# Attention feeding two feed-forward layers on one core: products with v as two halves of 64 columns, sums of the probabilities on GpSimd and by way of DMAs, preparation in fixed slots

## The chip, the cores and the metric

One core of one Trainium2 chip. The metric is the device time of one execution in microseconds (us). The engines are TensorE (PE; PEld is its weight load), VectorE (DVE), ScalarE (ACT), GpSimd (POOL) and SyncE (SP), which here only issues DMAs.

## The reference: what is computed

Attention with a mask by clusters, and two feed-forward layers on its output (numpy, cut):

```python
# q, k, v: (2, 8, 768, 64); centroids: (8, 16, 64)
q_assign = argmax(einsum('bhsd,hcd->bhsc', q_n, c_n), axis=-1)   # q_n, c_n: normalised rows
k_assign = argmax(einsum('bhsd,hcd->bhsc', k_n, c_n), axis=-1)
mask = q_assign[:, :, :, None] == k_assign[:, :, None, :]
scores = where(mask, q @ k.T / 8, -1e9)
attn = exp(scores - max(scores));  attn = attn / (sum(attn) + 1e-9)
x = (attn @ v) as (1536, 512)
h = maximum(x @ w_in, 0);  x = h * h @ w_out          # layer 1: 512 -> 2048 -> 512
h = x @ w2_in;  out = h * cos(h) @ w2_out             # layer 2
```

## The kernel before

The 16 (batch, head) problems go as 8 **pairs** of heads; the two heads of a pair (`j`) lie in partitions 0 to 63 and 64 to 127. Every engine's order is written out by hand: Python loops append instructions, and each engine runs its own list in order.

**Steps.** The main loop counts `g`. At step `g`, `scores(g)` makes the scores of one tile of 128 keys against 384 queries (half a head, `HALF`) for both heads: 8 products on TensorE, each on one half of the array's rows, then one `exp` on ScalarE into a tile `p` (L400). In the same step `s_max(g + 9)` (`LEAD` is 9) makes scores of a later tile in the other orientation (L350), and VectorE takes row maxima of them (L353). A pair is 12 steps, so the loop has 96 with scores. On odd steps `pv` multiplies two finished tiles `p` with `v`.

**Banks.** Scores, maxima and every preparation share three PSUM `unit`s, handed out in turn. A step's use of a unit waits for whoever read it three uses earlier, in most cases the maximum of the step before (DVE) or the `exp` (ACT).

**pv before.** `p` is the stationary operand (128 keys x 128 queries), `vv` the moving one: 64 columns of v and one column of ones, so that column 65 collects the sum of the probabilities. Both heads and three query tiles lie side by side in one bank `o_ps[hf]`, which a product with `zeros` opens. `divide` (7 steps after a half begins) adds 1e-9 to the sums, inverts them and multiplies on VectorE. `combine` (a step later) transposes the result on TensorE; ScalarE writes the high part `xh`, VectorE the rest `xl`.

**Preparation** of a pair (`prep`, a table by step): load q and k, squares and sums (`norm_sq`, `norm_sum`), 14 small VectorE instructions for the inverse norms (`norm_inv`), transposes (`transpose_in`) with two copies on ScalarE (`h` rounded, `f` exact), the remainder (`low_part`), similarities to the centroids in f32 (`sims`), the argmax as one-hot rows (`cluster`, `one_hot`), and DMAs that lay rows into `xq`, `xk`, `yk`, which `s_max` and `scores` read.

**Weights.** Each feed-forward weight is split into two parts by 6 VectorE instructions and an ACT copy (`w_split`, L135 to L144). The first 7 half-tiles (`n_early`) are loaded and split during attention, one instruction a step; the other 25 of layer 1 are loaded after `att.close()`, when attention's buffers are given back, and are split during the first 15 steps of the layer.

Of the kernel before, what the change touches and what calls it, by code (L numbers as in the profile page):

```python
# [33 lines left out]
def tile_kernel(ctx: ExitStack, tc: tile.TileContext, q, k, v, centroids, w1i, w1o, w2i, w2o, out):  # L34
# [22 lines left out]
    ps = ctx.enter_context(tc.tile_pool(name="ps", bufs=1, space=PSUM))  # L57

# [10 lines left out]
    zeros = perm.tile([P, 2 * HT * (D + 1)], BF16, name="zeros")  # L69
    nc.gpsimd.memset(zeros, 0.0)  # L70
# [107 lines left out]

    vv = [ap.tile([P, NT, 2, D + 1], F32, name=f"vv{i}") for i in range(2)]

    def load_raw(n, names):
        b, hp = pairs[n]
        for nm in names:
            if nm == "v":
                t = vv[n % 2][:, :, :, :D]
            else:
                t = prepp.tile([P, NT, 2, D], F32, tag=f"raw{nm}", name=f"raw{nm}{n}", bufs=2)
            src = {"q": q, "k": k, "v": v}[nm]
            for j in range(2):
                nc.sync.dma_start(t[:, :, j, :], src[b, 2 * hp + j].rearrange("(p t) d -> p t d", t=NT))  # L190
            raw[n, nm] = t
# [49 lines left out]
    def transpose_in(n, x):  # L241
        d = pd[n]
        u = unit()
        for t in range(NT):
# [3 lines left out]
            )  # L248
        d["h" + x] = ap.tile([P, S], F32R, tag="h" + x, name=f"h{x}{n}", bufs=3)
        d["f" + x] = prepp.tile([P, S], F32, tag="f" + x, name=f"f{x}{n}")  # L250
        d["l" + x] = ap.tile([P, S], F32R, tag="l" + x, name=f"l{x}{n}", bufs=3)
        nc.scalar.copy(halves(d["h" + x]), wide(u))
        nc.scalar.copy(halves(d["f" + x]), wide(u))
        d["t" + x] = u
# [67 lines left out]
    def one_hot(n):  # L322
        d = pd[n]
        u = unit()
        for t in range(NT):
# [4 lines left out]
            )  # L330
        ot = prepp.tile([2 * GC, S], F32R, tag="ot", name=f"ot{n}")
# [424 lines left out]
```

## Time and profile before

| | |
|---|---|
| median of 3 runs | 990.65 us (987.68 to 992.36) |
| the profiled execution | 982.26 us, of which the span is 980.5 us |
| PE busy | 917.2 us, 94% of the span |
| DVE busy | 601.8 us, 61% |
| ACT busy | 366.7 us, 37% |
| POOL busy | 28.3 us, 3% |
| mean granted TensorE clock | 0.926 of full speed |

The profiled execution is 0.85% below the median. Busy shares are averages over stages with different limits: preparation of the first pair (to about 29 us), the pairs of attention (to about 405 us), and the two layers.

### The profile page before, as it was taken

The page shows a single profiled execution, that of the slowest core. Times are in us where ns is not written, and L with a number is a line of the kernel's source. Part 1 is how long each engine was busy: PE and PEld are TensorE (multiplying, and loading weights), DVE is VectorE, ACT ScalarE, POOL GpSimd, SP SyncE. Part 2 cuts the span into 40 slices and gives each one's busy share as a digit, 9 for nine tenths or more (in the row PEclk, how much of TensorE's full clock was granted, in tenths as well). Part 3 has the DMA queues.
Part 4 walks back from the last instruction along what each step waited for, and adds up shares of the span by engine and source line. Part 5 has one row for each costly group of instructions (what it writes and reads, how often), then busy time and mean ns, then how long its engine had stood idle before and what let it go on. Part 6 is the DMA issues. An engine that isn't in the chain of part 4 may idle for free.

```text
span 980.5 us, 12966 instructions
## 1 busy us (share of the span) xinstructions
PE 917.2 (94%) x5097; PEld 759.4 (77%) x5097; DVE 601.8 (61%) x1159; ACT 366.7 (37%) x580; POOL 28.3 (3%) x58
## 2 busy tenths in 40 slices
PE   5699999999999999999879999999899999999997
PEld 5488888888888888887568888887677778887886
DVE  6775656453545442299972112899899885666655
ACT  2252525251525233344433334444433343333332
POOL 4000000000000000010000000000012000000000
PEclk6587979795979799999999999999999999999999
DMA  8240313121211110590000001665200010001001
GB/s 239 57 90 13 78 25 66 29 62 29 61 25 34 29 30 9 179 357 1 1 1 1 1 0 47 192 192 173 85 1 1 1 43 1 1 1 43 0 1 43
DMA packets 65934, 54.89 MB, mean 56 GB/s; under 512 B 40784, under 2 KB 58192, under 8 KB 65872
## 3 DMA queue, kind: packets, MB, share of 16 engines
q1 hardware_dynamic: 65872, 54.05, 19.5%
q8 instruction: 40, 0.66, 0.3%
q14 instruction: 22, 0.18, 0.1%
HBM read 43.02 MB, written 3.15 MB: 47 GB/s over the span
## 4 chain that ended last, share of the span: by engine, by line
PE 64%; DVE 25%; ACT 4%; issue 4%; DMA 3%; SPq 0%; POOL 0%; DVEq 0%; ACTq 0%
PE unit L503 17%; PE o_ps L418 15%; PE unit L396 10%; PE unit L564 8%; PE o_ps L564 7%; DVE top L143 3%; PE unit L350 3%; DVE aux L141 3%; DVE aux L144 2%; PE unit L279 2%; DVE ewr L542 2%; ACT p L400 2%; DVE w L136 2%; DMA wraw<-in_moe_w_out_dram 2%; DVE aux L140 2%
## 5 line engine op out<-in xcount | busy, mean ns | idle before, releaser
L503 PE MATMUL unit<-xh,w 128*128 128x512 f32 x768 | 258.2, 397 | 15.1 <-DVE ews L525 9.8
L503 PEld LDWEIGHTS unit<-xh,w 128*128 128x128 f32 x768 | 144.7, 189 | 55.9 <-DVE ews L525 13.7
L418 PEld LDWEIGHTS o_ps<-vv,p 128*128 128x128 f32 x1152 | 151.1, 212 | 8.5 <-issue 8.4
L418 PE MATMUL o_ps<-vv,p 128*128 128x65 f32 x1152 | 154.3, 296 | 0.0
L503 PE MATMUL unit<-xl,w 128*128 128x512 f32 x384 | 151.8, 395 | 0.0
L400 ACT ACTIVATE p<-unit 128x768 f32<-128x768 f32 x96 | 77.8, 813 | 184.3 <-PE unit L396 178.8
L353 DVE TENSOR_REDUCE m<-unit 128x2 f32<-128x768 f32 x96 | 91.4, 952 | 87.5 <-PE unit L350 87.3
L542 DVE TENSOR_TENSOR ewr<-ews,ewr 128x512 fp32r<-128x512 f32 x83 | 57.0, 687 | 79.0 <-ACT ewr L520 77.0
L503 PEld LDWEIGHTS unit<-xl,w 128*128 128x128 f32 x384 | 72.5, 189 | 15.6
L564 PE MATMUL unit<-ewr,w 128*128 128x512 f32 x288 | 76.7, 402 | 6.9 <-ACT w L135 6.9
L564 PE MATMUL unit<-w,ewr 128*128 128x512 f32 x288 | 75.1, 395 | 1.0 <-DVE ewr L542 1.0
L564 PE MATMUL o_ps<-ewr,w 128*128 128x512 f32 x288 | 75.7, 399 | 0.0
L564 PE MATMUL o_ps<-w,ewr 128*128 128x512 f32 x288 | 74.7, 394 | 0.0
L529 ACT ACTIVATE ews<-ews,hpi 128x512 f32<-128x512 f32 x48 | 34.8, 724 | 96.7 <-DVE ews L528 96.7
L564 PEld LDWEIGHTS unit<-ewr,w 128*128 128x128 f32 x288 | 53.5, 189 | 22.3 <-ACT w L135 9.4
L135 ACT CAST w<-top 128x512 fp32r<-128x512 f32 x64 | 39.7, 620 | 75.6 <-DVE top L143 74.1
L564 PEld LDWEIGHTS o_ps<-ewr,w 128*128 128x128 f32 x288 | 55.1, 191 | 13.4
L564 PEld LDWEIGHTS unit<-w,ewr 128*128 128x128 f32 x288 | 54.0, 188 | 14.3 <-DVE ewr L542 1.4
L537 DVE TENSOR_TENSOR ews<-unit,ews 128x512 f32<-128x512 f32 x48 | 33.2, 691 | 51.2 <-ACT ews L533 45.2
L564 PEld LDWEIGHTS o_ps<-w,ewr 128*128 128x128 f32 x288 | 54.1, 188 | 13.0
L518 ACT ACTIVATE ews<-unit 128x512 f32<-128x512 f32 x48 | 28.7, 598 | 86.9 <-PE unit L503 86.9
L396 PE MATMUL unit<-hq,hk 64*128 64x384 f32 x192 | 46.0, 476 | 13.4 <-DVE m L353 10.9
(145 smaller groups left out, 1148.0 us busy)
## 6 DMA issues: line engine op xcount, KB each, us to landing
wraw<-in_moe_w_in_dram SPq DMA_DIRECT2D x32, 512.0 KB, 4.5
wraw<-in_moe_w_out_dram SPq DMA_DIRECT2D x32, 512.0 KB, 4.2
rawq<-in_q_dram SPq DMA_DIRECT2D x16, 192.0 KB, 4.1
rawk<-in_k_dram SPq DMA_DIRECT2D x16, 192.0 KB, 4.3
vv<-in_v_dram SPq DMA_DIRECT2D x16, 192.0 KB, 3.2
out_dram<-outs SPq DMA_DIRECT2D x12, 256.0 KB, 2.2
xk<-hk SPq DMA_DIRECT2D x16, 96.0 KB, 2.1
xq<-lq SPq DMA_DIRECT2D x16, 96.0 KB, 2.2
```

The source lines that it names most:

```text
L135: nc.scalar.copy(w[:, 0], top.bitcast(F32))
L141: cost(690, lambda: ve.scalar_tensor_tensor(restf, low, 2.0**-32, rest, ALU.mult, ALU.add)),
L143: cost(690, lambda: ve.scalar_tensor_tensor(top, high, 0xC0000000, top, ALU.bitwise_and, ALU.bitwise_or)),
L353: nc.vector.tensor_reduce(d["m"][:, i, :, kh], u[:, :, :HALF], AX, ALU.max)
L396: nc.tensor.matmul(u[:, j, :HALF], lhsT=a[r, ks], rhs=b[r, qs], start=(p == 0), stop=(p == len(ops) - 1))
L400: nc.scalar.activation(t, u[:, :, :HALF], AF.Exp, scale=SCALE)
L418: nc.tensor.matmul(o[:, i, j], lhsT=t[:, j, i * P : (i + 1) * P], rhs=vv[n % 2][:, kt, j], start=False, stop=(kt == NT - 1 and i == HT - 1 ...
L503: nc.tensor.matmul(ph, lhsT=w[:, a, :], rhs=x[blk][:, a, :], start=(a == i == 0), stop=(a == KD - 1 and i == 2))
L529: nc.scalar.activation(e2, e2, AF.Sin, bias=hpi)
L537: nc.vector.tensor_tensor(e2, ph, e2, ALU.mult)
L542: e.tensor_tensor(al, e2, ah.bitcast(F32), ALU.subtract)
L564: nc.tensor.matmul(y, lhsT=a, rhs=b, start=(f == 0 and i == 0), stop=(f == NF - 1 and i == 2))
```

## The change

It does five things.

1. `pv` takes v as the stationary operand (64 columns of one head) and `p` as the moving one (384 queries). Head 0 writes partitions 0 to 63 of `o_ps[hf]`, head 1 partitions 64 to 127. There is no column of ones, no `zeros`, and no transpose in `combine`.
2. `add_up` adds the six tiles `p` of a half on GpSimd into `acc` (5 additions of 128x768). `sums` multiplies `acc` with a tile of ones; `move_sums` copies the result (ACT) and DMAs a row of it over 32 partitions; `invert` works on the 64x12 numbers, DMAs them to DRAM, and DMAs each row back over 64 partitions (`rb`). `divide` is one multiplication, 13 steps after the half begins. `xl` is made on GpSimd.
3. `sims` works on `h` and `l` parts: three products per tile in place of an f32 one, q and k in one unit. The copies `f` go.
4. The preparation has slots within a step (PRE: ahead of the scores, PROD: behind pv, POST: last), and starts 5 steps earlier.
5. `n_early` is 8. Early splits run one instruction a step up to step 0, then 2 in 5 steps; late ones by a rule that gives two half-tiles to each of the layer's steps 2 to 10 and one to steps 11 to 16.

```diff
     def load_raw(n, names):
...
-                t = vv[n % 2][:, :, :, :D]
+                t = ap.tile([P, NT, 2, D], F32, tag="rawv", name=f"rawv{n}", bufs=2)
...
-    def sims(n, x):
...
+    def sims(n):
+        d = pd[n]
+        u = d["sim"] = unit()
+        hp = pairs[n][1]
+        for i, x in enumerate("qk"):
+            for t in range(NT):
+                ts = slice(t * P, (t + 1) * P)
+                for p, (a, c) in enumerate(((d["h" + x], cbh), (d["l" + x], cbh), (d["h" + x], cbl))):
+                    nc.tensor.matmul(
+                        u[:, i, t * GC : (t + 1) * GC], lhsT=a[:, ts], rhs=c[:, hp, :], start=(p == 0), stop=(p == 2)
+                    )
...
+    def add_up(u_):
+        hb, kt = divmod(u_, NT)
+        if kt == 0:
+            return
+        if kt == 1:
+            accs[hb] = ap.tile([P, 2, HALF], F32, tag="acc", name=f"acc{hb}", bufs=2)
+            nc.gpsimd.tensor_tensor(accs[hb], ptiles[u_ - 1], ptiles[u_], ALU.add)
+        else:
+            nc.gpsimd.tensor_tensor(accs[hb], accs[hb], ptiles[u_], ALU.add)
 
     def pv(u_):
...
-        for i in range(HT):
-            for j in range(2):
-                nc.tensor.matmul(
-                    o[:, i, j], lhsT=t[:, j, i * P : (i + 1) * P], rhs=vv[n % 2][:, kt, j],
-                    start=False, stop=(kt == NT - 1 and i == HT - 1 and j == 1),
-                )
+        for j in range(2):
+            nc.tensor.matmul(
+                o_ps[hf][j * D : (j + 1) * D, :HALF], lhsT=raw[n, "v"][:, kt, j, :], rhs=t[:, j],
+                start=(kt == 0), stop=(kt == NT - 1),
+            )
+    def sums(hb):
+        u = su[hb] = unit()
+        acc = accs.pop(hb)
+        for j in range(2):
+            nc.tensor.matmul(u[j * D : (j + 1) * D, 0, :HALF], lhsT=ones, rhs=acc[:, j], start=True, stop=True)
+    def move_sums(hb):
+        u = su.pop(hb)
+        t = ap.tile([P, HALF], F32, tag="st", name=f"st{hb}")
+        nc.scalar.copy(t, u[:, 0, :HALF])
+        give(u)
+        r = inv[hb] = ap.tile([2 * R, GR], F32, tag="r", name=f"r{hb}", bufs=2)
+        for j in range(2):
+            nc.sync.dma_start(r[j * R : (j + 1) * R], t[j * D : j * D + 1].rearrange("o (p c) -> o p c", c=GR))
+    def invert(hb):
+        b, hp = pairs[hb // 2]
+        r = inv.pop(hb)
+        nc.vector.tensor_scalar(r, r, 1e-9, None, ALU.add)
+        nc.vector.reciprocal(r, r)
+        row = dram.tile([2, HALF], F32, tag="row", name=f"row{hb}", bufs=2)
+        nc.sync.dma_start(row.rearrange("j (p c) -> (j p) c", c=GR), r)
+        rb = rbs[hb] = ap.tile([P, HALF], F32, tag="rb", name=f"rb{hb}", bufs=2)
+        for j in range(2):
+            nc.sync.dma_start(rb[j * D : (j + 1) * D], row[j : j + 1, :].broadcast_to([D, HALF]))
     def divide(hb):
-        o = o_view(hb % 2)
...
+        x = xs[hb] = ap.tile([P, HALF], F32, tag="x", name=f"x{hb}", bufs=2)
+        nc.vector.tensor_tensor(x, o_ps[hb % 2][:, :HALF], rbs.pop(hb), ALU.mult)
...
             nc.scalar.copy(dst, src)
-            nc.vector.tensor_tensor(xl[blk][:, hp, off : off + w], src, dst.bitcast(F32), ALU.subtract)
+            nc.gpsimd.tensor_tensor(xl[blk][:, hp, off : off + w], src, dst.bitcast(F32), ALU.subtract)
...
-                for i in range(1 + (idx % 3 != 1)):
+                for i in range(-(-len(to_split[0]) // (NF + 1 - idx))):
...
+    prep = [
+        (-22, PRE, load_raw, "qk"),
+        (-17, PROD, transpose_in, "q"),
...
+        (-13, PRE, norm_sum, "k"),
+        (-12, PRE, norm_inv),
+        (-11, PROD, transpose_in, "k"),
+        (-10, PRE, high_part, "k"),
+        (-10, POST, low_part, "k"),
+        (-9, PROD, sims),
+        (-8, PRE, scale_sims),
+        (-7, PRE, cluster, 0, 1),
+        (-6, PRE, cluster, 1, 3),
+        (-5, PRE, cluster, 3, 4),
+        (-4, PRE, cluster, 4, 5),
+        (-3, PRE, stage),
+        (-3, PROD, one_hot),
+        (-2, PRE, stage_oh),
...
+    finish = [
+        (8, PROD, sums),
+        (9, PRE, move_sums),
+        (11, PRE, invert),
+        (13, PRE, divide),
+        (13, POST, combine),
+    ]
```

**TensorE, the products of a pair in the middle of attention.** `p` are tiles of probabilities, `hq` to `yk` the operands of scores (L396, now L411) and maxima (L350, now L360), `xt` the divided result, `cb` the centroids. Before:

```order
L418 MATMUL o_ps_66<-vv_128,p_1003 128x65 x6
L418 MATMUL o_ps_66<-vv_128,p_1042 128x65 x6
L396 MATMUL unit_63<-hq_350,hk_377 128x384 x2
L396 MATMUL unit_63<-hq_350,lk_379 128x384 x2
L396 MATMUL unit_63<-xq_122,xk_124 128x384 x2
L396 MATMUL unit_63<-lq_352,yk_126 128x384 x2
L350 MATMUL unit_64<-hk_669,hq_610 128x384 x2
L350 MATMUL unit_64<-xk_123,xq_121 128x384 x2
L442 MATMUL unit_65<-ident,xt_1123 128x128 x3
L279 MATMUL unit_63<-cb,fq_1028 128x32 x6
```

And now:

```order
L433 MATMUL o_ps_68<-p_673,rawv_399 64x384 x2
L433 MATMUL o_ps_68<-p_703,rawv_399 64x384 x2
L411 MATMUL unit_65<-hq_220,hk_268 128x384 x2
L411 MATMUL unit_65<-hq_220,lk_276 128x384 x2
L411 MATMUL unit_65<-xq_123,xk_125 128x384 x2
L411 MATMUL unit_65<-lq_238,yk_127 128x384 x2
L360 MATMUL unit_66<-hk_414,hq_345 128x384 x2
L360 MATMUL unit_66<-xk_126,xq_124 128x384 x2
L446 MATMUL unit_67<-acc_612,ones 64x384 x2
```

Six products of 65 columns for each tile of keys became two of 384; the transposes of `xt` went and `sums` came.

**VectorE, from the end of a pair's norms (`nr`) on.** L353 (now L363) are the maxima for which TensorE waits. Before:

```order
L226 RECIPROCAL nr_1836<-na_1942 128x24
L353 TENSOR_REDUCE m_1795<-unit_64 128x2
L450 TENSOR_TENSOR xl_109<-unit_65,xh_106 128x384
L284 TENSOR_TENSOR sm_1977<-unit_63,nr_1836 128x192
L362 TENSOR_REDUCE m_1986<-m_1795 128x6
L353 TENSOR_REDUCE m_1795<-unit_65 128x2
```

And now:

```order
L224 RECIPROCAL nr_1688<-na_1807 128x24
L363 TENSOR_REDUCE m_1841<-unit_67 128x2 x2
L143 TENSOR_SCALAR top_208<-wraw_40_234 128x512
L460 TENSOR_SCALAR r_1824<-r_1824 64x12
L461 RECIPROCAL r_1824<-r_1824 64x12
L363 TENSOR_REDUCE m_1841<-unit_67 128x2
L257 TENSOR_TENSOR lk_1915<-unit_65,hk_1881 128x768
```

The maxima still stand behind the whole run of norms; the similarities (`sm`) moved away from it, and the inversion of sums (`r`) and the remainder `lk` moved into the steps behind.

**SyncE, the DMAs around the rows of the next pair.** `r`, `row`, `rb` are the sums on their way, `xk` to `ot` the operands of the next pair's maxima. Before:

```order
L377 DMA lq_1029<-mr_1652 32x384 x2
L269 DMA xk_123<-hk_1500 32x768 x2
L269 DMA xq_121<-lq_1445 32x768 x2
L269 DMA yk_125<-hk_1500 32x768 x2
L338 DMA xq_121<-ot_1715 16x768 x2
L338 DMA xk_123<-ot_1715 16x768 x2
```

And now:

```order
L455 DMA r_1631<-st_1629 32x1x12 x2
L392 DMA lq_921<-mr_1657 32x384 x2
L463 DMA row_1692<-r_1631 64x12
L466 DMA rb_1694<-row_1692 64x384 x2
L268 DMA xk_125<-hk_1478 32x768 x2
L268 DMA xq_123<-lq_1323 32x768 x2
L268 DMA yk_127<-hk_1478 32x768 x2
L348 DMA xq_123<-ot_1751 16x768 x2
L348 DMA xk_125<-ot_1751 16x768 x2
```

Ahead of the rows of the next pair now stand `row`, which waits for VectorE, and `rb`, which waits for `row` to land.

## Rows read from the trace of the kernel before

**Rows 1.** The page's first part: busy us, share of the span, instructions.

```profile
PE 917.2 (94%) x5097; PEld 759.4 (77%) x5097; DVE 601.8 (61%) x1159; ACT 366.7 (37%) x580; POOL 28.3 (3%) x58
```

**Rows 2.** Busy time by stretch: length, busy of each engine (instructions), then PEclk, DMA.

```profile
128.87:142.52 13.65, 13.65 (x72) 12.60 (x70) 5.06 (x11) 2.35 (x4) 0.00 (x0) 0.50 0.00 0
142.52:176.65 34.13, 31.75 (x282) 27.65 (x282) 22.13 (x52) 15.55 (x24) 0.00 (x0) 1.00 0.31 64
...
135.68:182.88 47.20, 44.81 (x346) 39.67 (x346) 26.38 (x59) 17.89 (x27) 0.00 (x0) 0.86 0.22 47
```

**Rows 3.** Timeline of PE, two steps at full clock: start, us, instruction.

```profile
101.06 2.89 PE L418 MATMUL o_ps<-vv,p 128*128 128x65 f32 x24
103.88 0.45 PE L396 MATMUL unit<-hq,hk 64*128 64x384 f32 x2
104.17 0.34 PE L396 MATMUL unit<-hq,lk 64*128 64x384 f32 x2
104.34 0.34 PE L396 MATMUL unit<-xq,xk 64*128 64x384 f32 x2
...
105.14 0.55 PE L442 MATMUL unit<-ident,xt 128*128 128x128 f32 x3
105.82 0.45 PE L396 MATMUL unit<-hq,hk 64*128 64x384 f32 x2
...
107.07 0.34 PE L413 MATMUL o_ps<-zeros 128*128 128x390 bf16 x1
```

**Rows 4.** Groups by line: busy us, mean ns, idle before.

```profile
L418 PE MATMUL o_ps<-vv,p 128*128 128x65 f32 x1152 | 154.3, 296 | 0.0
```

**Rows 5.** The chain that ended last, a stretch of layer 1: start, us, what.

```profile
536.22 2.73 PE unit L503 x12
```

**Rows 6.** Timeline of PE and DVE around the norms of a pair.

```profile
124.04 0.17 DVE L214 TENSOR_SCALAR na<-nr 128x24 int32<-128x24 int32 x1
...
124.78 1.53 PE L279 MATMUL unit<-cb,fq 128*128 128x32 f32 x12
...
126.84 0.30 DVE L226 RECIPROCAL nr<-na 128x24 f32<-128x24 f32 x1
...
127.34 0.94 DVE L353 TENSOR_REDUCE m<-unit 128x2 f32<-128x768 f32 x1
...
128.34 0.44 PE L396 MATMUL unit<-hq,hk 64*128 64x384 f32 x2 [2.04 <-DVE m L353]
```

**Rows 7.** Timeline of DVE and POOL in layer 2.

```profile
710.02 0.68 DVE L525 SCALAR_TENSOR_TENSOR ews<-ews,unit 128x512 f32<-128x512 f32 x1
710.16 1.27 POOL L542 TENSOR_TENSOR ewr<-ews,ewr 128x512 fp32r<-128x512 f32 x1 [6.83 <-ACT ewr L538]
710.73 1.25 DVE L526 SCALAR_TENSOR_TENSOR ews<-ews 128x512 f32<-128x512 f32 x1
```

**Rows 8.** DMA issues by line (count, KB each, median us to landing).

```profile
rawk<-in_k_dram SPq DMA_DIRECT2D x16, 192.0 KB, 4.3
...
lq<-mr SPq DMA_DIRECT2D x32, 48.0 KB, 1.9
```

**Rows 9.** Timeline of SP: how long it issues two DMAs.

```profile
337.07 1.17 SPq L269 DMA_DIRECT2D xk<-hk  x2
```

**Rows 10.** Timeline of the first pair's preparation.

```profile
12.20 2.74 PE L279 MATMUL unit<-cb,fq 128*128 128x32 f32 x12 [0.36 <-POOL xq L487]
...
28.82 1.29 PE L350 MATMUL unit<-xk,xq 64*128 64x384 f32 x2 [3.92 <-DMA xk<-ot]
```

**Rows 11.** Timeline from the last exp to the layer's step 16.

```profile
402.29 1.51 ACT L400 ACTIVATE p<-unit 128x768 f32<-128x768 f32 x2 [2.78 <-PE unit L396]
402.75 0.35 SPq L115 DMA_DIRECT2D wraw<-in_moe_w_out_dram  x1
...
414.09 0.83 DVE L140 TENSOR_SCALAR aux<-wraw 128x512 uint32<-128x512 uint32 x1
...
508.09 0.40 PE L503 MATMUL unit<-xh,w 128*128 128x512 f32 x1
```

More of the change, by code (lines that the diff above doesn't have):

```diff
@@ L68, in tile_kernel @@
     nc.vector.tensor_copy(identr, ident)
-    zeros = perm.tile([P, 2 * HT * (D + 1)], BF16, name="zeros")
-    nc.gpsimd.memset(zeros, 0.0)
+    ones = perm.tile([P, D], F32, name="ones")
+    nc.gpsimd.memset(ones, 1.0)
     rank = perm.tile([P, NC], BF16, name="rank")
@@ L176, in head_rows @@
         return slice(j * D + part * R, j * D + (part + 1) * R)
-    vv = [ap.tile([P, NT, 2, D + 1], F32, name=f"vv{i}") for i in range(2)]
     def load_raw(n, names):
@@ L248, in transpose_in, with high_part @@
             )
+        d["t" + x] = u
+    def high_part(n, x):
+        d = pd[n]
         d["h" + x] = ap.tile([P, S], F32R, tag="h" + x, name=f"h{x}{n}", bufs=3)
[L250 to L254, printed above, removed]
+        nc.scalar.copy(halves(d["h" + x]), wide(d["t" + x]))
     def low_part(n, x):
         d = pd[n]
+        d["l" + x] = ap.tile([P, S], F32R, tag="l" + x, name=f"l{x}{n}", bufs=3)
         nc.vector.tensor_tensor(
@@ L438, in combine @@
         b, hp = pairs[n]
-        u = unit()
-        xt = xts.pop(hb)
-        for i in range(HT):
-            nc.tensor.transpose(u[:, 0, i * P : (i + 1) * P], xt[:, i].rearrange("p j d -> p (j d)"), ident)
+        x = xs.pop(hb)
         c = hf * HALF
@@ L676, in tile_kernel @@
     tops.extend(early_w.tile([P, DM], U32, name=f"top{i}") for i in range(2))
-    for g in range(-LEAD - 12, NU + 3):
-        calls = []
-        for n in range(NPAIR):
-            for f, *a in prep.get(g - (SP * n - LEAD), ()):
-                if not (n == 0 and f is load_raw and a[0] == "qk"):
-                    calls.append((f, n, a))
-        for f, n, a in calls:
-            if f in first_ops:
-                f(n, *a)
+    G0 = -LEAD - 17
+    for g in range(G0, NU + 8):
         if g == NU:
@@ L688, in tile_kernel @@
                 free_units.remove(u)
+        run(g, PRE)
         if 0 <= g < NU:
@@ L696, in tile_kernel @@
                     pv(u_)
-        for hb in range(2 * NPAIR):
-            if g - 6 * hb == 7:
-                divide(hb)
-            elif g - 6 * hb == 8:
-                combine(hb)
-        for f, n, a in calls:
-            if f not in first_ops:
-                f(n, *a)
-        if g == -LEAD - 9:
+        run(g, PROD)
+        run(g, POST)
+        if 0 <= g - 1 < NU:
+            add_up(g - 1)
+        if g == G0 + 1:
             for f, h in early_halves:
                 w_load(0, f, (h,))
-        if -LEAD - 6 <= g:
-            if not split_q and len(to_split[0]) > 2 * NF - n_early:
-                split_q.extend(next_split(0)[0])
-            if split_q:
-                split_q.pop(0)()
+        if g >= G0 + 4:
+            for i in range(1 if g < 0 else g % 5 < 2):
+                if not split_q and len(to_split[0]) > 2 * NF - n_early:
+                    split_q.extend(next_split(0)[0])
+                if split_q:
+                    split_q.pop(0)()
         if g == SP * (NPAIR - 1) - LEAD:
```

101 lines of the change are left out of this document (51 added, 50 removed).

## The prediction

> **What bounds the kernel now.** The page's first part comes first: TensorE is busy for 94% of the span, VectorE for 61%, GpSimd for 3% [rows 1]. TensorE is the bound, so the next questions are what a pair of heads costs it and at which clock. The view by stretches answers both [rows 2]. A whole pair lasts 47.2 us, of which TensorE is busy for 44.8, so it idles for 2.4. Its mean clock is 0.86, which is two levels: 13.65 us at half (1.2 GHz) and some 34 at full (2.4 GHz). A stretch of 13.65 us at half does the work of 6.8 at full, so the low clock costs a pair 6.8 us. At full clock without idling a pair would last 47.2 - 2.4 - 6.8 = 38.0.
>
> The timeline shows why the clock falls [rows 6]. VectorE runs the 14 instructions of a pair's norms from 124.04 to 127.14 in one piece, a split and the row maximum wait behind them, and TensorE idles for 2.04 us for that maximum. The clock is at half from 128.87 on.
>
> Next, what pv costs. Two tiles of keys take from 101.06 to 103.88, 2.82 us for 24 instructions, 0.118 each; each f32 product is two instructions, 1152 for 576 calls [rows 3, 4]. The similarities move 32 columns in place of 65 and take 1.53/12 = 0.127 each [rows 6]. The cost therefore does not follow the columns that move: it is that of loading 128 columns of weights.
>
> **Products with v.** Each tile now has 2 products of 384 columns, 4 instructions, with 64 columns of weights. No row shows f32 with so many columns. Below, 384 rounded columns take 0.17 (a run of 12 of 512 takes 2.73, so 0.228 each, and 384/512 of it) [rows 5]. Above, 65 columns take no more than 0.118, so 384 no more than 0.69. I take 0.34, twice the rounded product: the weights are visibly split in two halves, so I charge the moving side two passes as well. It is nearest to the first row, whose product has the same length.
>
> Do the two column halves run at once? The only halves in the trace are row halves: two products of 384 on them are issued every 0.17 us (104.17 to 104.34), where one after another would take 0.34, so they overlap [rows 3]. I take the same for columns. With the order a, a', b, b' of each tile, a' runs beside b and b' beside the next a, so two tiles take 5 slots of 0.34 = 1.7, and 8 slots = 2.7 if nothing overlaps. Against 2.8 that saves 1.1 or 0.1; six times a pair, 6.7 or 0.6. Whatever the columns do, a rival below takes the other end.
>
> The Trainium skill (TensorE: Matmul & The Clock Gate, section The mechanism) says that a weight load overlaps with running products only when its row group differs. Column halves share all rows, so by that rule their loads would stand in the open; at 0.06 each (half of 0.118) that is 8 x 0.06 more for two tiles, and the saving of 1.1 falls to 0.6. The trace speaks against it in general: the 12 products of 128 rows at 0.228 leave no room for their weight loads.
>
> **Other work of TensorE per pair.** Similarities: 36 products in place of 24, at 0.127: +1.5. Sums: two a pair at 3 slots = 1.0 each: +2.0 (2.7 without overlap). The transposes of the result go (105.14 to 105.82 with its wait, 0.6 each), and two `zeros` (0.18 each) [rows 3]: -1.5. Together with pv: -6.7 + 1.5 + 2.0 - 1.5 = -4.7, or +2.1 without overlap. At full clock, unhindered: 38.0 - 4.7 = 33.3.
>
> **GpSimd and what it does to VectorE.** GpSimd takes 1.27 for 128x512 [rows 7], so 1.9 for 128x768: ten additions are 19 us of a pair, with `xl` 21. That is no bound by itself, and each addition is due two steps before its sum. But the same rows show a price. L525 reads PSUM and starts beside an addition: 0.68, undisturbed. L526 reads two operands from SBUF, starts at 710.73 and takes 1.25; it ends 0.55 after the addition's end at 711.43. Such an instruction waits for the addition. Of that kind are the norms, four of the cluster instructions, and half of the splits. Row maxima and `low_part` read PSUM and are free, but stand behind them in VectorE's list.
>
> The worst place is the norms: 3.1 us, with the row maximum of that step behind them [rows 6]. Between the end of one maximum on TensorE and its need of the one behind the norms lie two scores with maxima (2 x 1.26, 103.88 to 105.14 [rows 3]), sums (1.0) and pv (1.7), 5.2 in all; the reductions ahead and behind take 0.94 each on VectorE, with their waits 2.1. That leaves 3.1: the norms just fit where nothing holds them. Additions come nearly one a step, 1.9 in some 3; one or two fall into it. I take 3 us of idling there (0 to 5.8, no addition to three). At the cluster instructions, the splits and the inversions (some 10 places, tight in three of the steps) I take 2.5 more (0 to 8).
>
> The Trainium skill (SBUF — State Buffer, section Who interferes with whom) goes further than these rows: a copy or an operation with a constant in VectorE's two-port modes contends as well, and the second to issue blocks fully. By that rule all 14 norms count, not 9, and with additions back to back only one gets through between two; the idling at the norms would be its upper end, 5.8, and the pair 2.8 longer. No row here shows it.
>
> **DMAs.** A DMA is issued in 0.6 (two in 1.17) and lands some 2 later [rows 8, 9]. From `invert` to `divide` there are `row` (2.0), two issues of `rb` (1.2) and a landing (2.0): 5.2 with VectorE's part, against two steps of 2 x 33.3/12 = 5.6. On SyncE `rb` waits for `row` to land, and the ten DMAs of the next pair's rows (6 us of issue) stand behind it; for every other half, q and k of a later pair (4.3 to land) stand ahead. The next pair's first maximum waits for the last of these. I take 2.5 of idling a pair (0 to 5). Idling in all: 3 + 2.5 + 2.5 = 8.
>
> **The clock.** It falls now behind 2.04 us of idling. There will be such gaps in some pairs. The half stretch should be shorter, since products that stream 384 columns replace those that wait for weights: I take 2.5 lost a pair (0 to 6.8, as now). A pair: 33.3 + 8 + 2.5 = 43.8, 3.4 less than now. From 50 to 405 us there are 6.25 pairs with all of this: -21.
>
> **The ends.** The last nine steps have no maxima: two of them take 2.8 + 2 x 0.7 = 4.2 now, and then at least two additions, 3.9; the dozen steps before have maxima but hardly any preparation and gain up to 1.1 for two: -5 in all (0 to -10). Start: the first pair's similarities run at 0.23 each (2.74/12) [rows 10], half of the 12 more in the open, and norms and three splits now stand ahead of `low_part`: +4 (0 to 8) on the first maximum, now at 28.82.
>
> Entry to layer 1: the last weights are issued now at 402.75, a microsecond before the last exp ends at 403.8 [rows 11]. Then they stand behind the last `rb`: GpSimd's lag and addition 4.5, sums 1, copy 0.5, `r` 2.5, `row` and issues 3.7, so 12 behind it; with 4.5 to land, the first late split starts 16.7 behind the exp, where it now starts at 414.09, 10.3 behind. That is +6.4. One half-tile less is -3.8: 94 us for 25 of them until step 16 at 508.09. Two a step early, one a step late lets TensorE run the last six steps without waiting: -3. Sum 0 (-4 to +8).
>
> **The sum.** -21 - 5 + 4 + 0 = -22 us on the profiled 982.3, so 960. That execution lies 0.85% below the median of 990.65; on the median the forecast is 968.
>
> **The rivals.** *Nothing held.* Additions miss VectorE's runs, the clock stays up: idling 4, clock 0, a pair 37.3, 9.9 less: -62 - 5 + 4 = -63, 928. For it: the norms fit into their slot. Against: GpSimd is busy for more than half of the time.
>
> *Column halves one after another.* TensorE +2.1: 40.1, with longer steps that hide more (idling 4, clock 2.5): 46.6, so -4 in all, 0 at the end, +4 at the start: no change, 991. No row shows column halves at once.
>
> *VectorE behind the additions: slower.* Nine or ten additions a pair each hold VectorE for about half their length as L526 was held (0.56 of 1.27), and the norms for three: idling 11, and the clock falls in every pair for as long as now, 6.8: a pair of 51.1, +3.9 x 6.25 = +24, with the ends 1016. It decides from idling plus clock of 13.9 a pair on. For it: rows 7, and that the norms' slot has no slack. Against: whenever TensorE stalls, no exp follows and GpSimd runs dry, which frees VectorE.
>
> **Chances.** The forecast's case 0.40 (950 to 986), nothing held 0.12, halves in sequence 0.22 (975 to 1005), VectorE held 0.26 (995 to 1030). 0.5%, 5 us, is about what a measurement tells from no change. Faster: 0.36 + 0.12 + 0.08 = 0.56. Same: 0.04 + 0.07 + 0.02 = 0.13. Slower: 0.07 + 0.24 = 0.31. The range leaves out the outer half of the first and the outer third of the last rival: 932 to 1018.
>
> **What would show it.** Right: the f32 products of 384 columns in pairs, 17 us of pv a pair falling to 10; norms of 4 to 7 us with their two-operand instructions lengthened up to 1.9; a pair near 44. Wrong: instructions of pv spaced 0.34 with no overlap; or a mean clock below 0.93 with idling of over 11 a pair; or waits for `rb` or `xk` of several us at the maxima; or a start after 36 us.

## The result, and the profile after

| | before | after |
|---|---|---|
| median | 991.5 us (987.68 to 994.86, 4 runs) | 956.54 us (953.85 to 961.0, 4 runs) |
| ratio | | 0.9653, 95% interval 0.9599 to 0.9707 |
| the profiled execution | 982.26, span 980.5 | 954.84, span 953.1 |

The forecast was 968 on the median and 22 us less on the profiled executions; these lie 27.4 apart. Runs of the kernel before scatter from 967.67 to 994.86 over the measurements below, and a ratio is taken over a kernel's undisturbed runs alone (without 928.17 in one addition of five, whose other three have the median 917.97), so the experiments are compared by their own medians, with the ratio of each to the kernel before beside it. Two kernels below that have the time of after (958.06 and 957.13) have ratios of 0.9775 and 0.9708: the gain is 2 to 3.5%, and which of these the one measurement of after can't tell.

The page's first part, to be read beside [rows 1]:

```profile
PE 852.2 (89%) x4425; PEld 640.4 (67%) x4425; DVE 639.8 (67%) x1104; ACT 362.0 (38%) x581; POOL 193.8 (20%) x160
```

TensorE's busy time fell by 65 us, but the span only by 27: it now idles for 11% of the time. Where that is shows best between milestones found in both timelines: the first scores of the first pair (49.30 before, 58.28 after), those of the seventh (340.10, 322.10), the last scores (402.03, 375.45), step 16 of layer 1 (508.09, 485.04) and the end.

| stretch | before | after | difference |
|---|---|---|---|
| to the first scores | 49.3 | 58.3 | +9.0 |
| six pairs | 290.8 | 263.8 | -27.0 |
| the last two pairs | 61.9 | 53.4 | -8.6 |
| last scores to step 16 | 106.1 | 109.6 | +3.5 |
| to the end | 472.4 | 468.1 | -4.3 |

Busy time by stretch, columns as in [rows 2], of before:

```profile
49.30:340.10 290.80, 275.76 (x2041) 243.06 (x2039) 156.83 (x347) 106.27 (x160) 0.00 (x0) 0.83 0.21 44
```

and of after:

```profile
58.28:322.10 263.82, 221.89 (x1544) 143.60 (x1542) 193.61 (x302) 100.26 (x156) 121.79 (x75) 0.89 0.23 55
...
162.10:168.90 6.80, 4.31 (x22) 3.43 (x22) 3.55 (x9) 0.95 (x2) 0.60 (x1) 0.50 0.56 128
171.79:175.70 3.91, 3.91 (x37) 3.91 (x36) 1.29 (x2) 0.68 (x1) 0.00 (x0) 1.00 0.20 55
```

Such a row gives a pair's account. Idling is the length less PE's busy time, over six: 15.0/6 = 2.5 before, 41.9/6 = 7.0 after. The clock costs what its mean lacks to 1, times the length: 0.17 x 290.8/6 = 8.2 before, 0.11 x 263.8/6 = 4.8 after. What is left of a pair is work at full clock: 48.5 - 2.5 - 8.2 = 37.8 before, 44.0 - 7.0 - 4.8 = 32.2 after. Idle time at half clock counts twice in this account and makes the work look smaller: 5.4 us of it in six pairs of after, 0.5 a pair.

A timeline of all engines after, in several places (start, us, instruction; in brackets the idling before it and what ended it):

```profile
36.79 0.99 PE L360 MATMUL unit<-xk,xq 64*128 64x384 f32 x2 [4.43 <-DMA xk<-ot]
...
155.49 4.17 POOL L426 TENSOR_TENSOR acc<-acc,p 128x768 f32<-128x768 f32 x2
...
156.06 1.71 DVE L212 TENSOR_SCALAR na<-nr 128x24 int32<-128x24 int32 x1
...
157.12 0.20 PEld L433 LDWEIGHTS o_ps<-p,rawv 128*64 128x64 f32 x4 [0.18 <-issue]
...
157.50 0.14 PEld L433 LDWEIGHTS o_ps<-p,rawv 128*64 128x64 f32 x2 [0.18 <-issue]
...
157.82 0.14 PEld L433 LDWEIGHTS o_ps<-p,rawv 128*64 128x64 f32 x2 [0.18 <-issue]
...
158.01 1.69 DVE L217 TENSOR_TENSOR na<-nr,ny 128x24 f32<-128x24 f32 x1
...
160.91 1.80 POOL L426 TENSOR_TENSOR acc<-acc,p 128x768 f32<-128x768 f32 x1 [1.25 <-ACT p L415]
161.04 1.70 DVE L218 SCALAR_TENSOR_TENSOR na<-na,ny 128x24 f32<-128x24 f32 x1
...
163.65 0.89 DVE L363 TENSOR_REDUCE m<-unit 128x2 f32<-128x768 f32 x1
...
164.59 0.69 PE L360 MATMUL unit<-hk,hq 64*128 64x384 f32 x2 [4.75 <-DVE m L363]
...
171.79 0.28 PE L279 MATMUL unit<-cbh,hq 128*128 128x32 f32 x1
...
175.72 0.36 PE L279 MATMUL unit<-cbl,hk 128*128 128x32 f32 x1
176.01 0.69 PE L411 MATMUL unit<-hq,hk 64*128 64x384 f32 x2
...
181.35 0.87 PE L446 MATMUL unit<-acc,ones 128*64 128x384 f32 x4
182.14 0.44 PE L411 MATMUL unit<-hq,hk 64*128 64x384 f32 x2
...
190.03 1.51 PE L433 MATMUL o_ps<-p,rawv 128*64 128x384 f32 x8
191.48 0.44 PE L411 MATMUL unit<-hq,hk 64*128 64x384 f32 x2
...
375.71 1.51 ACT L415 ACTIVATE p<-unit 128x768 f32<-128x768 f32 x2 [0.23 <-PE unit L411]
...
376.66 7.52 POOL L426 TENSOR_TENSOR acc<-acc,p 128x768 f32<-128x768 f32 x4
...
384.23 0.87 PE L446 MATMUL unit<-acc,ones 128*64 128x384 f32 x4 [1.87 <-POOL acc L426]
...
395.74 0.56 DVE L470 TENSOR_TENSOR x<-o_ps,rb 128x384 f32<-128x384 f32 x1 [5.44 <-DMA rb<-row]
...
397.65 0.55 DVE L141 TENSOR_SCALAR aux<-wraw 128x512 uint32<-128x512 uint32 x1 [1.36 <-DMA wraw<-in_moe_w_in_dram]
```

Products of two tiles with v take 1.45 (190.03 to 191.48) where they took 2.82 [rows 3]. Taken singly, the eight instructions start in four pairs, 7 ns apart within a pair and 0.32 to 0.37 from pair to pair (190.035 and 190.042, then 190.408, 190.731, 191.053). The norms, 3.1 us in one piece before [rows 6], take 7.6 here (156.06 to the maximum at 163.65): three instructions of 0.17 to 0.18 are stretched to 1.7, each beside an addition on GpSimd, and TensorE idles for 4.75 us for the maximum behind them. The clock falls within that stop, at 162.10, and is at half for 6.8 us. The 36 similarities (171.79 to 176.01) run at full clock but for the last: at 175.74 the clock falls again, for 3.4 us, though TensorE had not idled since the stop ended at 164.59. So it is in each of the six pairs: a fall between 1.3 us ahead of the end of the similarities and 0.7 behind it, without a stop before it, for 3.4 us (once 6.8). These are 23.9 us at half clock in six pairs, and half of that is 2.0 of the 4.8 that the clock costs a pair.

What TensorE waited for between 60 and 405 us (total, times, longest):

```profile
PE unit L360 <- DVE m L363: 27.9, 17, 4.8
PE unit L360 <- DMA xk<-ot: 5.4, 9, 1.5
```

And groups by line (busy, mean ns):

```profile
L426 POOL TENSOR_TENSOR acc<-acc,p 128x768 f32<-128x768 f32 x64 | 118.6, 1853 | 65.1 <-ACT p L415 62.5
L363 DVE TENSOR_REDUCE m<-unit 128x2 f32<-128x768 f32 x96 | 90.5, 944 | 49.7 <-PE unit L360 49.4
...
L217 DVE TENSOR_TENSOR na<-nr,ny 128x24 f32<-128x24 f32 x24 | 11.9, 494 | 0.8
L212 DVE TENSOR_SCALAR na<-nr 128x24 int32<-128x24 int32 x8 | 6.4, 796 | 0.0
```

The maxima themselves (L363), which read PSUM, are no longer than before (0.94 in [rows 6]); they stand behind what is held.

### The profile page after: what moved, and what is told of

It reads as the page before. It is cut to its first block, busy times and chain, and to the rows that moved or that the text cites. A ratio compares the mean times of both kernels' runs of the same rounds, so it can differ in the third digit from the quotient of the medians.

```text
span 953.1 us, 11830 instructions
## 1 busy us (share of the span) xinstructions
PE 852.2 (89%) x4425; PEld 640.4 (67%) x4425; DVE 639.8 (67%) x1104; ACT 362.0 (38%) x581; POOL 193.8 (20%) x160
## 4 chain that ended last, share of the span: by engine, by line
PE 49%; DVE 35%; DMA 6%; issue 4%; SPq 2%; ACT 2%; DVEq 0%; POOL 0%; ACTq 0%
PE unit L538 18%; PE unit L599 8%; PE o_ps L599 8%; PE unit L279 4%; PE unit L411 4%; DVE m L363 4%; PE o_ps L433 3%; DVE top L144 3%; DVE aux L142 3%; PE unit L360 3%; DMA rb<-row 2%; DVE w L137 2%; DMA row<-r 2%; DVE aux L141 2%; DVE aux L145 2%
## 5 line engine op out<-in xcount | busy, mean ns | idle before, releaser
L538 PEld LDWEIGHTS unit<-xh,w 128*128 128x128 f32 x768 | 146.8, 191 | 63.2 <-DVE ews L560 15.2
L426 POOL TENSOR_TENSOR acc<-acc,p 128x768 f32<-128x768 f32 x64 | 118.6, 1853 | 65.1 <-ACT p L415 62.5
L363 DVE TENSOR_REDUCE m<-unit 128x2 f32<-128x768 f32 x96 | 90.5, 944 | 49.7 <-PE unit L360 49.4
L577 POOL TENSOR_TENSOR ewr<-ews,ewr 128x512 fp32r<-128x512 f32 x13 | 16.7, 1286 | 329.5 <-ACT ewr L573 319.6
L433 PE MATMUL o_ps<-p,rawv 128*64 128x384 f32 x384 | 82.0, 553 | 0.0
L360 PE MATMUL unit<-hk,hq 64*128 64x384 f32 x192 | 40.2, 412 | 27.9 <-DVE m L363 27.9
L599 PEld LDWEIGHTS o_ps<-w,ewr 128*128 128x128 f32 x288 | 54.1, 188 | 11.8
```

Of the source, the lines that this page charges most:

```text
L360: nc.tensor.matmul(u[:, j, :HALF], lhsT=a[r, qs], rhs=b[r, ks], start=(p == 0), stop=(p == 1))
L363: nc.vector.tensor_reduce(d["m"][:, i, :, kh], u[:, :, :HALF], AX, ALU.max)
L426: nc.gpsimd.tensor_tensor(accs[hb], accs[hb], ptiles[u_], ALU.add)
L433: nc.tensor.matmul(o_ps[hf][j * D : (j + 1) * D, :HALF], lhsT=raw[n, "v"][:, kt, j, :], rhs=t[:, j], start=(kt == 0), stop=(kt == NT - 1),)
L538: nc.tensor.matmul(ph, lhsT=w[:, a, :], rhs=x[blk][:, a, :], start=(a == i == 0), stop=(a == KD - 1 and i == 2))
L577: e.tensor_tensor(al, e2, ah.bitcast(F32), ALU.subtract)
```

## Experiments

The theory to test: TensorE's smaller work at v carries the gain, and the additions on GpSimd give a good part of it back, by holding VectorE and through it TensorE and its clock. The rivals: slots and similarities carry it; the idling comes from the order of VectorE's list or from DMAs; column halves run at once, or they don't.

The accounts of a pair, by the method above (first scores of the first to those of the seventh pair), each from one row of that view, of which some are shown below:

| kernel | median us | pair | idling | clock | work |
|---|---|---|---|---|---|
| before | 991.5 | 48.5 | 2.5 | 8.2 | 37.8 |
| after | 956.5 | 44.0 | 7.0 | 4.8 | 32.2 |
| old products | 975.1 | 46.2 | 1.2 | 6.0 | 39.0 |
| one addition of five | 920.4 | 38.3 | 3.2 | 3.1 | 32.0 |
| neighbours on one half | 958.1 | 45.1 | 7.6 | 5.9 | 31.6 |
| norms in pieces | 974.9 | 46.9 | 7.5 | 7.0 | 32.4 |
| additions in halves | 957.1 | 43.7 | 6.0 | 5.7 | 32.0 |
| division a step later | 980.8 | 47.9 | 8.9 | 8.1 | 30.9 |
| additions on VectorE | 931.4 | 39.7 | 3.5 | 3.6 | 32.6 |

The kernel with neighbours on one half has the time of after and differs from it by 0.6 to 1.1 in these columns: as much is within what two traces of like kernels show. With the division a step later 13.8 us of idling lie at half clock, 1.2 a pair, so its work is nearer to 32 than to 30.9.

**The old products in the new slots.** `pv`, `divide` and `combine` of before, with `vv` and `zeros`:

```diff
-        (8, PROD, sums),
-        (9, PRE, move_sums),
-        (11, PRE, invert),
-        (13, PRE, divide),
-        (13, POST, combine),
+        (7, PROD, divide),
+        (8, PROD, combine),
...
-        if 0 <= g - 1 < NU:
-            add_up(g - 1)
```

> The changed kernel with the products, the division and the transposes of before; slots, similarities and the pacing of the splits stay as changed. If the new products carry the gain: TensorE gets 8 us a pair more (two tiles 2.82 in place of 1.45, no sums, transposes back), the idling behind additions and rb goes (from 6.8 a pair to 2 or 3), so a pair of 46 to 48 us in place of 44.0, and 965 to 985 us in all. If the slots and the similarities carried the gain, it stays at 957 or falls below.

975.13 us (970.6 to 978.61, 10 runs), ratio 0.9997 (0.9963 to 1.0031). By stretch:

```profile
57.90:335.20 277.30, 269.94 (x2105) 237.49 (x2103) 153.01 (x342) 97.82 (x147) 0.00 (x0) 0.87 0.22 46
```

and TensorE's timeline at the end of a pair's similarities:

```profile
127.64 0.38 PE L281 MATMUL unit<-cbh,lk 128*128 128x32 f32 x1
...
130.38 5.38 PE L434 MATMUL o_ps<-vv,p 128*128 128x65 f32 x24
```

As the theory had it. The other parts of the change together are worth nothing that this measurement can tell: in the profile they win 2.3 a pair and lose 8.6 until the first scores (57.9). The way of the products is worth 18.6 us beside after, 17.1 beside the kernel with neighbours on one half from the same measurement. In a pair it takes 6.8 of work away and brings back 5.8 of idling. The clock's 6.0 a pair come without stops here: in all six pairs it falls within 1 us of the end of the similarities (at 127.62 in the rows above), where TensorE had not idled, and stays at half for 10.2 to 13.7 us, so that products with v in it take 5.4 where they take 2.9 at full clock [rows 3].

**One addition of five.**

```diff
-        if kt == 0:
+        if kt != 1:
             return
```

> One addition of a half's five is left (16 in place of 80), so the sums cover two tiles of six. If the additions hold VectorE and through it TensorE: the norms take about 3 us everywhere, TensorE's idling falls from 6.8 a pair to 2 or 3 and the clock with it, a pair of 39 to 40.5 us, in all 920 to 940. If the idling comes from the order of VectorE's list and from DMAs: a pair stays at 43 to 44 and the time above 950.

920.37 us (914.29 to 928.17), ratio 0.9377 (0.9304 to 0.945).

```profile
58.10:287.90 229.80, 210.37 (x1544) 139.27 (x1542) 150.13 (x302) 100.54 (x156) 33.58 (x27) 0.92 0.27 63
```

The work of a pair is the same to 0.2 us, idling falls by 3.8 and the clock's share by 1.7. TensorE's waits for the row maxima (L360 for `m`) fall from 27.9 us to 3.3. The falls of the clock at the end of the similarities stay, 3.4 us in each of the six pairs. The additions that were left out cost 36 us, more than the forecast's whole gain. VectorE is busy for 43 us less in this stretch (193.6 to 150.1), and nothing was taken from its list: that is time for which it was held.

**Neighbouring products on one column half.**

```diff
-            for u_ in (g - 3, g - 2):
-                if 0 <= u_ < NU:
-                    pv(u_)
+            for j in range(2):
+                for u_ in (g - 3, g - 2):
+                    if 0 <= u_ < NU:
+                        pv(u_, j)
```

> Products of one head for both tiles of keys first, then those of the other, so that neighbours in the list write the same column half. If column halves run at once: eight instructions of 0.32 one after another, 2.6 us for two tiles in place of 1.45, 48 times 1.15 is 55, of which idling hides some: 980 to 1010. If an instruction takes 0.16 and nothing runs at once: 1.45 as now and 957, no change.

958.06 us (954.24 to 959.2), ratio 0.9775 (0.9718 to 0.9833). Its timeline:

```profile
196.88 1.52 PE L432 MATMUL o_ps<-p,rawv 128*64 128x384 f32 x8
198.33 0.44 PE L411 MATMUL unit<-hq,hk 64*128 64x384 f32 x2
```

1.45 again: the order of the halves is of no account for the time. The time is that of the second expectation, but the trace speaks against its reason. Here too the eight instructions start in pairs, now 13 to 14 ns apart within a pair (196.882 and 196.895) and again 0.32 to 0.37 from pair to pair. Each product is two instructions, so the next one for the other column half stands two places on in the list of after and four places on here. For the row halves of the scores it is the next in the list, and there a pair starts 3 ns apart. The distance within a pair grows with these places, 3, 7 and 13.5 ns (the last two in nine pairs of ten of either trace). So a pair is most likely one instruction on either column half, the two running at once for some 0.32, in both orders of the list; eight in sequence would not start two by two. The first expectation took for granted that neighbours on one half keep the other half waiting, and that did not hold. This is read from starts: no run used one column half alone.

**The norms in three pieces.**

```diff
-        (-12, PRE, norm_inv),
+        (-12, POST, norm_inv, 0, 5),
+        (-11, POST, norm_inv, 5, 10),
+        (-10, POST, norm_inv, 10, 14),
```

> The 14 instructions of the norms go in pieces of 5, 5 and 4 at the end of three steps, with the row maxima between them. If the maximum behind the whole run is what TensorE waits for there (2.6 us a pair now, up to 4.8 at once) and the clock falls behind it: 3 to 5 us a pair less, 925 to 942. If VectorE loses as much wherever the pieces stand: no change, 952 to 960.

974.92 us (968.95 to 977.2, 10 runs), ratio 0.9931 (0.9886 to 0.9976): 18 slower than after, which neither side had foreseen. Timeline and stretches of its similarities (L281 here):

```profile
173.87 0.45 PE L362 MATMUL unit<-hk,hq 64*128 64x384 f32 x2 [1.86 <-DVE m L365]
...
175.53 0.28 PE L281 MATMUL unit<-cbh,hq 128*128 128x32 f32 x1 [1.05 <-DVE lk L259]
```

```profile
59.30:340.60 281.30, 236.37 (x1544) 158.39 (x1542) 188.06 (x302) 99.97 (x156) 121.66 (x75) 0.85 0.22 51
...
175.53:182.70 7.17, 7.17 (x36) 7.15 (x36) 1.14 (x2) 0.00 (x0) 0.00 (x0) 0.55 0.09 30
176.20:186.40 10.20, 10.20 (x50) 8.92 (x51) 2.91 (x7) 1.82 (x4) 0.86 (x2) 0.50 0.06 21
```

The long stop is gone, but the idling is not: it comes in smaller pieces, at the maxima and ahead of the similarities. The clock now falls as the 36 small products begin and stays at half for 10.2 us; they take 7.2 in place of 4.2 at full clock. So it is in five of the six pairs (0.5 to 0.8 us into the similarities); in the sixth it falls 1.8 ahead of them, for 13.7. In after the clock fell at 162.10, within the stop of 4.75 us, was back when the similarities came at 171.79, and fell again only at their end, for 3.4 us. Why it falls where it does no run tells; that the fall lands on the similarities and lasts is what the rows show.

**Additions in halves.**

```diff
-            nc.gpsimd.tensor_tensor(accs[hb], accs[hb], ptiles[u_], ALU.add)
+        first = ptiles[u_ - 1] if kt == 1 else accs[hb]
+        for j in range(2):
+            nc.gpsimd.tensor_tensor(accs[hb][:, j], first[:, j], ptiles[u_][:, j], ALU.add)
```

> Each addition of 128x768 goes as two of 128x384 (1.0 us each by the xl of that size, in place of 1.85), one for each head. If an instruction of VectorE waits only for the piece that runs and gets in before the next: it is held for at most 1.0, TensorE's idling between the first and the last score falls from 47 us to about 32 and the clock's share with it, 930 to 948 in all. If each piece holds the next instruction again, so that the sum of the waits stays: 950 to 962.

957.13 us (950.19 to 958.47), ratio 0.9708 (0.9637 to 0.9778): no change. Its timeline in a pair's norms:

```profile
157.75 4.30 POOL L426 TENSOR_TENSOR acc<-acc,p 128x384 f32<-128x384 f32 x4
...
159.26 0.92 DVE L213 TENSOR_SCALAR ny<-na 128x24 int32<-128x24 int32 x1
160.22 0.92 DVE L217 TENSOR_TENSOR na<-nr,ny 128x24 f32<-128x24 f32 x1
161.18 0.92 DVE L218 SCALAR_TENSOR_TENSOR na<-na,ny 128x24 f32<-128x24 f32 x1
```

The rival holds nearly: between two pieces GpSimd lets one instruction of VectorE through, and the next one waits for the next piece. More of them are held, for half as long. VectorE's busy time in the six pairs falls from 193.6 to 184.4 us, a fifth of the 43 for which it was held, and TensorE's wait for the maxima from 27.9 to 25.3; of that the time shows nothing.

**Additions on VectorE.**

```diff
-            nc.gpsimd.tensor_tensor(accs[hb], accs[hb], ptiles[u_], ALU.add)
+            nc.vector.tensor_tensor(accs[hb], accs[hb], ptiles[u_], ALU.add)
```

(and the first of each half likewise)

> The additions go to VectorE, at the same places in the order: 80 times about 0.95 (lq of 128x768), ten a pair. With one addition of five left the same stretch took 281 us in place of 317, with 23 us of idling in place of 47, so 24 of idling and 12 of clock are what GpSimd's additions cost. If holding is the dear part: VectorE gets busy for 230 of some 300 us, its own additions cost 10 to 25 of idling where they stand ahead of a maximum, 925 to 955 in all. If VectorE's list is the limit, whoever adds: 960 or more.

931.4 us (929.58 to 934.14), ratio 0.9463 (0.94 to 0.9526). Its additions, by line:

```profile
L426 DVE TENSOR_TENSOR acc<-acc,p 128x768 f32<-128x768 f32 x64 | 60.8, 950 | 1.6 <-ACT p L415 0.9 <-DVE acc L426 0.5
```

VectorE adds in 0.95 what GpSimd adds in 1.85, and busy for more of the span than before (70%) it still stops TensorE for half as long (3.5 a pair in place of 7.0). Holding was the dear part.

**The division a step later.**

```diff
-        (13, PRE, divide),
-        (13, POST, combine),
+        (14, PRE, divide),
+        (14, POST, combine),
```

> The division and what follows it come a step later (14 in place of 13). VectorE waits 36 us for rb in 13 waits of up to 5.4, with the maxima queued behind. If TensorE pays for a part of these: 5 to 10 us less, 945 to 952. If rb's wait falls into VectorE's slack: 953 to 960. The last half, behind which the layer starts, comes later by a piece of the layer's first products, at most 1 or 2 us.

980.8 us (974.29 to 987.22, 10 runs), ratio 0.9964 (0.9922 to 1.0005): 24 slower than after. Its timeline:

```profile
203.12 1.01 POOL L483 TENSOR_TENSOR xl<-x,xh 128x384 fp32r<-128x384 f32 x1 [9.27 <-ACT xh L482]
204.10 1.81 POOL L424 TENSOR_TENSOR acc<-p,p 128x768 f32<-128x768 f32 x1
205.99 5.70 POOL L426 TENSOR_TENSOR acc<-acc,p 128x768 f32<-128x768 f32 x3
...
214.01 0.69 PE L360 MATMUL unit<-hk,hq 64*128 64x384 f32 x2 [7.08 <-DVE m L363]
```

GpSimd idles for 9.27 us for `xh`, which comes from the later division, with the additions queued behind `xl`. Then four of them run in one piece, and the norms fall into it: 7.08 us of idling at once. To test that reading, the same with the additions on VectorE:

> The later division again, but with the additions on VectorE. With additions on GpSimd it cost 24 us; the trace had xl wait at the head of GpSimd's list and the additions behind it burst onto the norms (up to 7.1 us of idling there). If that burst was the cause, a later division costs nothing without additions on GpSimd: 926 to 937, beside 931.4. If the later division hurts by itself (units, maxima behind it): 945 to 960.

933.83 us (931.17 to 935.36), ratio 0.9538 (0.9448 to 0.9627), beside 931.4 without the later division. The burst on GpSimd was the cause; the two ranges overlap, so these runs show no price of the later division alone.

**Similarities in f32 from an exact copy.**

```diff
-                for p, (a, c) in enumerate(((d["h" + x], cbh), (d["l" + x], cbh), (d["h" + x], cbl))):
...
+                nc.tensor.matmul(
+                    u[:, i, t * GC : (t + 1) * GC], lhsT=d["f" + x][:, ts], rhs=cb[:, hp, :], start=True, stop=True
+                )
```

> Similarities in f32 from an exact copy, as before the change: 24 instructions of 0.127 a pair in place of 36 of 0.112, so 3.0 in place of 4.1 us, and two copies on ScalarE more (0.95 each). If the term of TensorE counts: 1.1 for each of seven pairs and 2 to 3 at the start, where they run at half clock, 945 to 950. If ScalarE's copies or the clock eat it: 953 to 962.

938.88 us (937.53 to 942.9), ratio 0.9544 (0.948 to 0.9607): 17.7 faster, outside of both expectations. By stretch from first scores to seventh pair, and the first maximum:

```profile
52.65:307.10 254.45, 213.34 (x1474) 135.13 (x1472) 194.45 (x298) 108.78 (x168) 121.64 (x75) 0.88 0.24 57
```

```profile
33.62 0.99 PE L361 MATMUL unit<-xk,xq 64*128 64x384 f32 x2 [4.35 <-DMA xk<-ot]
```

The first scores come 5.6 us sooner (52.65 beside 58.28) and the six pairs take 9.4 less, 1.6 each where TensorE's share is 1.1. The first maximum comes 3.2 sooner. A fall of the clock without a stop comes in one of the six pairs here, not in all, but other falls last longer, and the time at half clock is the same (60.4 us beside 59.4); what the rest of the gain is stays open.

**Both, and the way of the sums.** Additions on VectorE with f32 similarities:

> Additions on VectorE and f32 similarities together, the two that were faster alone (931.4 and 938.9 against 956.5). If they remove different things (held instructions; TensorE's work and the start): 931 - 18 = 913, 905 to 922. If both mostly remove the same clock loss: 924 to 932.

911.04 us (909.46 to 911.81), ratio 0.9306 (0.9222 to 0.939): the two gains add up. On top of it, the very last half inverted where it lies:

```diff
     def invert(hb):
+        if hb == 2 * NPAIR - 1:
+            nc.vector.reciprocal(rbs[hb], rbs[hb])
+            return
```

> As the first kernel of this call, but the sums of the very last half are inverted where they lie (128x384 on VectorE), without the DMAs r, row and rb; 1e-9 is not added there. The 24 columns of the norms take 0.30 and the 12 of r 0.22, so about 2.6 us for 384. If the late loads and splits of layer 1 wait for the last half's way through the DMAs (10 us from r to x): x comes 6 to 8 us sooner and the whole is 4 to 8 us faster than the first kernel. If the loads or the splits themselves pace the start of the layer: within 2 us of it.

905.36 us (901.28 to 905.69), ratio 0.924 (0.9152 to 0.9328), 5.7 faster.

```profile
334.02 1.51 ACT L416 ACTIVATE p<-unit 128x768 f32<-128x768 f32 x2 [0.99 <-PE unit L412]
...
344.24 2.55 DVE L464 RECIPROCAL st<-st 128x384 f32<-128x384 f32 x1 [2.86 <-ACT st L452]
...
347.40 0.42 DVE L141 TENSOR_SCALAR aux<-wraw 128x512 uint32<-128x512 uint32 x1
```

The last exp ends at 335.5, the first late split starts 11.9 behind it; in the kernel that this one is built on it was 19.8 (333.54 to 353.30), in after 20.4. The DMAs of the last half paced the entry to layer 1. And all halves without DMAs:

```diff
-        (11, PRE, invert),
+        (10, POST, invert, 0),
+        (11, POST, invert, 1),
+        (12, POST, invert, 2),
```

> All halves inverted where they lie, in three pieces of 128 columns at the ends of three steps; no r, row and rb, and 1e-9 is not added. VectorE gets some 2.2 us more a half, 35 in all, in pieces of 0.9; SyncE and VectorE lose the waits for rb. If the DMAs cost TensorE little (1.2 us a pair by its waits) beside the last half: 3 to 15 us slower than the kernel with the last half alone direct. If the waits for rb are dear: as fast as that one or up to 10 us faster.

902.24 us (898.12 to 905.34), ratio 0.9218 (0.9096 to 0.9339). The ranges of the two overlap: as fast as the one before, which is the second expectation. VectorE's added work and the waits that went about balance:

```profile
L458 DVE RECIPROCAL st<-st 128x128 f32<-128x128 f32 x48 | 45.0, 942 | 5.1 <-ACT st L452 5.1
```

The waits' own price can't be told from these 45 us of VectorE that replace them. Both kernels beat before and after.

## Why the prediction came out as it did

The forecast's case won, at 956.54 within its 950 to 986. That a pair of 44.0 stands beside the predicted 43.8 is luck: the sum had 1.1 too much work and 1.0 too much idling, and 2.3 too little for the clock. The step that failed is the clock's. By stretch the profiled executions differ by -27.0 in six pairs, -8.6, +9.0, +3.5 and -4.3, where the sum had -21, -5, +4 and 0.

- **The pair of before.** The pair that was read, 47.2 us, is one of the shorter; six take 48.5 on the mean. This step alone hides 1.3 x 6 = 8 us of gain.
- **Products with v.** Predicted 1.7 for two tiles, five slots of 0.34; measured 1.45. The starts bear out both guesses, as far as they tell: instructions go two by two, one on either column half, and a pair takes 0.32. But there are four pairs, not five slots. Saving a pair: 6 x 1.37 = 8.2 in place of 6.7.
- **The rule on weight loads** (the Trainium skill, TensorE: Matmul & The Clock Gate, The mechanism: a load overlaps with running products only when its row group differs; the same section also lets loads into a background weight buffer go ahead). The two halves share all rows, and by the first rule alone two tiles would take 0.48 more. Of eight loads four come at 157.12, two at 157.50 and two at 157.82: but for the first two, each is for a pair of products that starts later, and runs beside the pair before on the same rows. The pairs follow one another 0.32 apart, only the first step is 0.05 longer. The trace does not bear the first rule out here.
- **Other work.** A sum takes 0.79, not 1.0. The similarities take 4.2 where they took 2 x 1.53 [rows 6], +1.1 at full clock where +1.5 was taken. Work of a pair: 32.2, predicted 33.3.
- **Idling.** Predicted 8 a pair, measured 7.0. The six waits behind the norms are 4.77, 0.26, 4.75, 0.79, 4.09 and 0.96, 2.6 on the mean where 3 was taken; `xk` costs 0.9. The two-operand instructions are stretched to 1.7 as foreseen.
- **Operations with a constant** (the Trainium skill, SBUF — State Buffer, Who interferes with whom: they contend as well). The shift L212 took 1.71 at 156.06 and 0.80 on the mean, 0.40 with one addition of five. The trace agrees, and that one instruction gets through between two additions too. The norms idled for 2.6 and not 5.8 all the same, since GpSimd waits for the exp between additions (62.5 us for L426).
- **The clock.** Predicted 2.5 a pair, measured 4.8. The forecast had the clock fall behind gaps in TensorE's work. Falls at stops there are, and their stretches at half cost 2.8 a pair (34.1 us in six pairs), near what was taken. The 2.0 a pair at the end of the similarities, where TensorE had not idled, were put at nothing. That the half stretches would be shorter held: 3.4 to 6.8 us, where they were 13.7 to 23.9 in before and 10.2 to 13.7 with the old products in the new slots. What sets their length no run shows.
- **The ends.** Last steps: -5 predicted, -8.6 over the last two pairs. Start: +4 predicted, +8.0 at the first maximum (36.79 beside 28.82 [rows 10]), 3.2 of it gone with f32 similarities (33.62). Entry: 0 predicted, +3.5 measured; the first late split is 20.4 behind the exp (predicted 16.7). The last sum starts 7.0 behind the exp (4.5 predicted), and from there to the split it takes 13.4 (12.2 predicted). The four additions that are left then are the smaller part: with additions on VectorE and f32 similarities the sum starts 5.1 behind the exp, and the split is still 19.8 behind. The -4.3 from step 16 on was not predicted; no edit touches those instructions, and it stays open.
- **The rivals.** *Column halves one after another* is out: two tiles take 1.45, not the 2.7 of eight slots, and the starts come two by two. *VectorE held behind the additions* was the right mechanism: 36 us, of which the forecast's 8 of idling and the clock took account. It was to decide from 13.9 of idling and clock a pair on; after has 11.8, and the kernel with the later division, at 17.0, is back at the time of before (ratio 0.9964). That margin is thin: one entry of a table moved by a step crosses it.

## What to carry to other kernels

Before work goes to GpSimd, count which instructions of VectorE run beside it: those on SBUF alone, with two operands or a constant, wait for GpSimd's running instruction, however small they are, so that 64 additions of 1.85 us cost 36 us of the span here, and all 80 moved to the busier VectorE, at 0.95 each, gave 25 back. Cutting the work into pieces did not help here (957.1), and an instruction ahead of it in GpSimd's list that comes late packs the pieces onto whatever VectorE does next. Read a stage's length as a mean over all its turns, not from one. And look up what TensorE did before each fall of the clock: here two fifths of what it cost came with the similarities and without a stop, for which a sum that looks at stops alone has no term.

## What the runs showed of the hardware

- GpSimd and VectorE take turns by instruction: beside additions of 1.85 us one instruction of 0.18 is stretched to 1.7 and the next is not; beside pieces of about 1.0 it is 0.92, three times in a row, and TensorE's waits for the maxima fall only from 27.9 to 25.3 us.
- A stretch at half clock costs by what lies in it: the 36 products of 32 columns took 4.2 us at full and 7.2 where it fell on them, and it lasted 10.2 us there, not 6.8. Spreading one stop over three steps made the kernel 18 us slower.
- The clock also falls where TensorE does not idle: at the end of the 36 similarities in all six pairs of after (for 3.4 us, once 6.8), with one addition of five (3.4) and with the old products (10.2 to 13.7).
- Two f32 instructions of 384 columns with 64 columns of weights, which by their starts run side by side on the two column halves, take 0.32 at full clock, where two rounded ones on the two row halves take 0.17 [rows 3]; f32 with 65 or 32 moving columns and 128 columns of weights costs 0.12 to 0.13 an instruction [rows 3, 6].
- A reciprocal of 128x384 takes 2.55 us on VectorE, a multiplication of that size 0.56.
